# A two-part kernel on one core: each GpSimd operation also waits for the VectorE operation ahead of it in the kernel's own plan

## The chip, the core and the metric

The kernel runs on one core of a Trainium2 chip. A core has five engines with a queue of instructions each: TensorE (PE in the profile, with its weight loads as PEld), VectorE (DVE), ScalarE (ACT), GpSimd (POOL) and SyncE (SP), which here issues all DMAs. An engine takes its instructions in order and waits at an instruction until the semaphores that it names have reached given values. The metric is the device time of one execution in microseconds (us).

## The reference

The first half is a recurrence over 768 time steps, for 4 sequences of 8 heads with 48 values each; the second half is a gated feed-forward block over the result. Cut to what is computed:

```python
for t in range(S):                       # S = 768, state is D x D, D = 48
    cur = einsum('bhd,bhe->bhde', u[None] * kt, vt)
    y[:, :, t] = einsum('bhd,bhde->bhe', rt, state + cur)
    state = wt[..., None] * state + einsum('bhd,bhe->bhde', kt, vt)
x = y as [4, 768, 384]
h = gelu(x @ w_in)                       # 384 -> 1024, tanh form
u, v = h[..., :512], h[..., 512:]
v_n = (v - mean) / sqrt(var + 1e-6) * g_ln
v_s = einsum('ts,bsd->btd', w_sg, v_n) + b_sg[None, :, None]
out = x + (u * v_s) @ w_out
```

## The kernel before

The 768 steps of each of the 4 sequences are cut into 6 chunks of 128 steps, 24 chunks in all, and each chunk into two blocks of 64. Within a chunk the recurrence becomes matrix products: running products of the decays (`decays`, two scans on VectorE, L465 and L473 or L480), keys and queries multiplied by them (`decayed_k`, L505, and L482), the products of decayed queries and keys on TensorE (L563), masked on VectorE (`masked`, L640), and a state per block that is carried on (`state` and `decayed`, L654, L663, L670, L683). `own_weights` makes the term with `u`: from chunk 4 on two multiplications of 128x384 (L527, L529), a sum over them on VectorE (L532), and a product with a diagonal (L540).

The feed-forward half runs per half sequence in pieces: `v_piece` (TensorE, then a gelu on ScalarE, L863, the statistics by one-column steps L865 to L873, and the normalised piece split into a high and a low part, L882), `u_piece`, `gate_piece` (L918 to L924) and `out_piece` (L942). Products that need full precision are three TensorE matmuls, high by high, high by low and low by high (L840, L841, L842). Weights come as 64-bit numbers and are turned into high and low parts on the chip: `f64_weight` (L989, L991, L995, L997, and L1008, L1010) and `f32_weight` (L1038).

Nothing of the order is left to a scheduler. Each of these functions is a generator that yields one `Op` for each instruction or small group: the engines that may do it with a cost in us for each, what it waits for, and what it takes and frees. `Plan.run` picks, again and again, the operation that can end first by these costs, on the engine where it ends first, and lets the generator record its instructions. So the order of each queue and the choice between VectorE, GpSimd and ScalarE come from one planned timeline. An `Op` with `two=True` also uses a port that VectorE and GpSimd share in the plan (`Op.port`, `Plan.port`): in the plan such an operation on VectorE and any operation on GpSimd never overlap. On the chip nothing keeps this: an instruction waits only for its data and its buffers, and a GpSimd operation whose inputs are there starts at once, whatever VectorE was planned to do first.

Of the program that runs, GpSimd has 26 operations of preparation and then 110 that the plan places; VectorE has 571 operations.

Of the kernel before, what the change touches and what calls it, by code (L numbers as in the profile page):

```python
# [80 lines left out]
class Op:  # L81
# [3 lines left out]
    def __init__(self, on, after=(), take=(), free=(), done=None, kb=None, two=False, apart=False, small=False, slack=0.0, n=6):  # L85
        self.on, self.after, self.take, self.free, self.done, self.kb = on, after, take, free, done, kb
        self.two = two
        self.n = n
        self.slack = slack
        self.small = small  # L90
        self.apart = apart
# [6 lines left out]
class Event:  # L98
    t = None
# [36 lines left out]
class Plan:  # L136
# [4 lines left out]
    def __init__(self):  # L141
        self.engines = dict.fromkeys(("PE", "DVE", "ACT", "POOL", "SP"), 0.0)
        self.procs = []
        self.log = []
        self.dma = 0.0
        self.lanes = [0.0] * 8
        self.port = 0.0
        self.count = 0
        self.pe_last = self.pe_before = None
        self.pos, self.came = FETCH[2], [0.0, 0.0]  # L150

    def fetched(self, t, end, n):

        step = (end - t) / n
        late = 0.0
        for _ in range(n):
            self.pos += 1
            t += step
            if self.pos % 256 == 256 - FETCH[1]:
                self.came = [self.came[1], t + late + FETCH[0]]  # L160
            elif self.pos % 256 == 0:
                late += max(0.0, self.came[0] - t - late)
        return late
# [20 lines left out]
    def run(self):  # L184
        while True:
            best = {}
            for p in self.procs:
                op = p[3]
                if any(e.t is None for e in op.after) or any(len(s.free) < op.take.count(s) for s in op.take):
                    continue  # L190
                ready = max([p[2]] + [e.t for e in op.after] + [s.since(op.take.count(s)) for s in op.take])
                _, t, e = min((s + self.cost(op, e, s) + BIAS.get(e, 0.0), s, e) for e in op.on
                              for s in (max(ready, self.engines[e], self.port if op.port(e) else 0.0,
                                        self.lanes[0] if op.kb is not None else 0.0),))
                best.setdefault(e, []).append((t, p[0], p[4], p))
            if not best:
                break
            pick = None
            for e, c in best.items():
                t0 = min(x[0] for x in c)  # L200
                x = min((x for x in c if x[0] <= t0 + 0.02), key=lambda x: (x[1], x[0], x[2]))
                if pick is None or x[0] < pick[0]:
                    pick = (x[0], e, x[3])
            t, e, p = pick
            op = p[3]
            op.e, op.end = e, t + self.cost(op, e, t)
            if e == "PE":
                op.end += self.fetched(t, op.end, op.n)
            self.engines[e] = op.end
            if e == "PE":  # L210
                self.pe_before, self.pe_last = self.pe_last, op
            if op.port(e):
                self.port = op.end
            if op.kb is not None:
                self.dma = max(op.end + 1.6, self.dma) + op.kb / 330.0
                op.seen = self.dma + 0.5 + op.slack
                self.lanes = self.lanes[1:] + [self.dma + 0.5]
            else:
                op.seen = op.end + self.LAT.get(e, 0.2)
            op.got = [s.take() for s in op.take]  # L220
            for b in op.free:
                b.done(op.seen)
            if op.done is not None:
                op.done.t = op.seen
            if not op.apart:
                p[2] = op.seen
            self.log.append((t, op.end, e, p[0], p[1].__name__))
            self._next(p, op)
            if p[3] is None:
                self.procs.remove(p)  # L230
        assert not self.procs, [(p[0], p[1].__name__) for p in self.procs[:40]]
# [70 lines left out]
def rwkv_gmlp(ctx: ExitStack, tc: tile.TileContext, wpad, kr, vtok, ktok, vt, u, ucol, w_in, consts_, w_sgT, w_out, out):  # L302
    nc = tc.nc
# [84 lines left out]
    before, full, eye = (junk[:, i * 128:(i + 1) * 128] for i in range(3))  # L388
# [16 lines left out]
    plan = Plan()  # L405
    plan.engines.update(DVE=2.0, POOL=3.5, ACT=2.1, SP=0.8)
    PLANS.append(plan)
    steps = [(b, g) for b in range(B) for g in range(NC)]
    N = len(steps)

# [882 lines left out]
```

## Time and profile before

| what | value |
| --- | --- |
| median of 3 runs | 371.54 us (369.52 to 372.68) |
| the profiled execution, its own time | 372.92 us |
| its span in the profile | 371.2 us |
| busy: PE, PEld, DVE, ACT, POOL | 345.1, 312.5, 284.7, 199.6, 103.3 us |
| the chain that ended last, by engine | PE 69%, DVE 22%, issue 3%, DMA 2%, ACT 2% |

The profile is of one execution; the 1.7 us between its time and its span lie before the first and behind the last instruction of the program. Instructions are named by engine, line (L12 is line 12 of the kernel), operation and the tiles they write and read. "Idle before" names what ended the idle time of an engine just ahead of an instruction.

### The profile page before, as it was taken

To read this page: it belongs to the slowest core of one execution; us is meant where nothing else is said; L and a number is where in the kernel's file an instruction comes from. 1 tells how busy PE (TensorE), PEld (TensorE's weight loads), DVE (VectorE), ACT (ScalarE), POOL (GpSimd) and SP (SyncE) were. 2 spreads that over 40 slices of the span, in tenths; PEclk is the share of its full clock that TensorE was granted. 3 is DMA by queue.
4 is the path that set the end of the run, shared out by engine and by line. 5 is a ranking of instruction groups with operands and counts; after the bars stand their busy time and mean duration, and the time that the engine had idled before them with its cause. 6 is when DMAs were issued, how large, how long until landed. Compare 5 with 4: busy or idle time off the path is not lost.

```text
span 371.2 us, 10746 instructions
## 1 busy us (share of the span) xinstructions
PE 345.1 (93%) x4429; PEld 312.5 (84%) x4429; DVE 284.7 (77%) x571; ACT 199.6 (54%) x520; POOL 103.3 (28%) x140
## 2 busy tenths in 40 slices
PE   2899588899999999999999999999999999999991
PEld 2576367679999889989899988999999899999991
DVE  7997999999999999899999998545726354553350
ACT  2666567767644677687564577521256783521110
POOL 6221917045233564534122611121100120100000
PEclk9989999999999999999999999999999999999997
DMA  8889477542435826746346620120445431001002
GB/s 243 330 272 312 150 241 221 177 159 71 125 119 175 263 76 196 245 133 189 92 141 191 194 77 3 64 79 6 140 152 181 134 117 50 1 0 44 21 8 66
DMA packets 23432, 50.64 MB, mean 136 GB/s; under 512 B 3024, under 2 KB 11984, under 8 KB 23376
## 3 DMA queue, kind: packets, MB, share of 16 engines
q1 hardware_dynamic: 23376, 49.88, 42.2%
q8 instruction: 37, 0.61, 0.7%
q14 instruction: 19, 0.16, 0.1%
HBM read 43.97 MB, written 4.72 MB: 131 GB/s over the span
## 4 chain that ended last, share of the span: by engine, by line
PE 69%; DVE 22%; issue 3%; DMA 2%; ACT 2%; SPq 0%; DVEq 0%; ACTq 0%
PE m_ps L840 14%; PE m_ps L841 13%; PE m_ps L842 13%; PE resets L840 5%; PE resets L842 5%; PE resets L841 5%; PE a_ps L563 4%; PE y_ps L586 3%; PE y_ps L597 2%; DVE W L465 2%; PE y_ps L570 2%; DVE W L473 2%; DVE KR L505 2%; DVE a L640 1%; DMA W<-in_wpad 1%
## 5 line engine op out<-in xcount | busy, mean ns | idle before, releaser
L840 PE MATMUL m_ps<-wsgh,vn 128*128 128x384 f32 x144 | 49.4, 343 | 0.3 <-ACT u L896 0.3
L841 PE MATMUL m_ps<-wsgl,vn 128*128 128x384 f32 x144 | 48.4, 336 | 0.0
L842 PE MATMUL m_ps<-wsgh,vn 128*128 128x384 f32 x144 | 48.4, 336 | 0.0
L871 POOL TENSOR_TENSOR st<-st,mhalf 128x1 f32<-128x1 f32 x24 | 17.3, 721 | 76.4 <-DVE st L869 69.4
L491 ACT ACTIVATE junk<-W 128x1040 bf16<-128x1040 f32 x24 | 25.7, 1070 | 13.4 <-DVE W L480 5.2
L840 PEld LDWEIGHTS m_ps<-wsgh,vn 128*128 128x128 f32 x144 | 27.0, 188 | 1.6 <-ACT u L896 0.6
L840 PE MATMUL m_ps<-xT,winh 128*128 128x384 f32 x78 | 27.0, 346 | 0.6 <-ACT kt L309 0.6
L841 PEld LDWEIGHTS m_ps<-wsgl,vn 128*128 128x128 f32 x144 | 27.0, 188 | 0.5
L842 PEld LDWEIGHTS m_ps<-wsgh,vn 128*128 128x128 f32 x144 | 27.0, 187 | 0.0
L840 PE MATMUL m_ps<-g,wouth 128*128 128x384 f32 (+1 forms) x80 | 26.8, 335 | 0.0
L842 PE MATMUL m_ps<-g,woutl 128*128 128x384 f32 (+1 forms) x80 | 26.4, 330 | 0.0
L841 PE MATMUL m_ps<-g,wouth 128*128 128x384 f32 (+1 forms) x80 | 26.4, 330 | 0.0
L841 PE MATMUL m_ps<-xT,winh 128*128 128x384 f32 x78 | 26.2, 336 | 0.0
L842 PE MATMUL m_ps<-xT,winl 128*128 128x384 f32 x78 | 26.2, 336 | 0.0
L563 PE MATMUL a_ps<-KR 64*64 64x128 f32 (+1 forms) x768 | 22.9, 256 | 1.1 <-DVE S L654 1.0
L527 POOL TENSOR_TENSOR RK<-RK,flat 128x384 f32<-128x384 f32 x17 | 20.9, 1234 | 10.7 <-DVE resets L920 6.4
L922 ACT CAST g<-m_ps 128x384 fp32r<-128x384 f32 x24 | 11.4, 477 | 21.4 <-DVE m_ps L920 21.4
L586 PE MATMUL y_ps<-a,vtok 64*64 64x64 f32 x768 | 21.3, 224 | 1.1 <-DVE S L670 0.6
L842 PE MATMUL m_ps<-winh,xT 128*128 128x512 f32 x51 | 20.2, 396 | 2.3 <-ACT xT L309 2.3
L465 DVE TENSOR_TENSOR_SCAN W<-W,D 128x520 f32<-128x520 f32 x16 | 21.9, 1371 | 0.0
L586 PEld LDWEIGHTS y_ps<-a,vtok 64*64 64x64 f32 x768 | 16.1, 134 | 6.7 <-issue 3.6
L942 DVE TENSOR_TENSOR o<-m_ps,x 128x384 f32<-128x384 f32 (+1 forms) x20 | 10.4, 529 | 14.6 <-PE m_ps L842 10.3
(184 smaller groups left out, 1009.5 us busy)
## 6 DMA issues: line engine op xcount, KB each, us to landing
KR<-in_kr SPq DMA_DIRECT2D x24, 512.0 KB, 4.5
RK<-in_ktok SPq DMA_DIRECT2D x20, 384.0 KB, 3.6
W<-in_wpad SPq DMA_DIRECT2D x24, 260.5 KB, 3.0
vtok<-in_vtok SPq DMA_DIRECT2D x24, 192.0 KB, 3.4
out<-o SPq DMA_DIRECT2D x23, 192.0 KB, 1.9
vn<-in_w_in SPq DMA_DIRECT2D x6, 512.0 KB, 6.9
KR<-in_w_in SPq DMA_DIRECT2D x6, 512.0 KB, 4.3
g<-in_w_sgT SPq DMA_DIRECT2D x6, 384.0 KB, 5.4
```

What stands on the lines that cost most here:

```text
L465: nc.vector.tensor_tensor_scan(Suf[:, WL - 1:0:-1], W[:, WL - 1:0:-1], r_one if early else D1[:, WL - 1:0:-1], 0.0, ALU.mult, ALU.add)
L473: nc.vector.tensor_tensor_scan(W[:, at], W[:, at], r_two, 0.0, ALU.mult, ALU.add)
L491: nc.scalar.activation(junk.bitcast(BF16).rearrange("p (a x) -> p a x", a=2), both, AF.Square, accum_out=chk[:, n:n + 1])
L527: engine[op.e].tensor_tensor(t[:, 0], t[:, 0], u_bc, ALU.mult)
L563: nc.tensor.matmul(ps_[64 * c_:64 * c_ + 64, j, p * C:p * C + (2 * T if c_ < turn else T)], x.K[rows, at:at + T], r_, start=True, stop=True)
L586: m = nc.tensor.matmul(place(y, j, q, r, c_), x.V[64 * c_:64 * c_ + 64, h * D - up(p, j):h * D - up(p, j) + 64], x.a.tile[64 * c_:64 * c_ ...
L840: nc.tensor.matmul(ps, lh, rh, start=(i == 0), stop=False)
L841: nc.tensor.matmul(ps, lh, rl, start=False, stop=False)
L842: nc.tensor.matmul(ps, ll, rh, start=False, stop=(i == n - 1))
L871: nc.gpsimd.tensor_tensor(rstd, var, c.mhalf, ALU.pow)
L922: nc.scalar.copy(gh, ps)
L942: nc.vector.tensor_tensor(o.tile[:, 0:w], ps, h_.x.tile[:, i, at], ALU.add)
```

## The change

`Plan.run` gets two hooks: how many instructions have been recorded so far, and a function that is called after each planned operation. In the kernel this function keeps a list of all VectorE operations with their planned ends. For each planned GpSimd operation that starts at the planned time t it looks up the last VectorE operation of the list that ends by t, and adds a dependency: the first GpSimd instruction waits for that VectorE operation's last instruction. Costs, choices and the order of every queue stay as they are.

```diff
@@ Plan.__init__
+        self.behind = lambda op, n, t: None
+        self.traced = lambda: 0
@@ Plan.run
+            n = self.traced()
             self._next(p, op)
+            self.behind(op, n, t)
@@ rwkv_gmlp
+    wait = mybir.DependencyInfo(mybir.DependencyClass.Sync, mybir.DependencyReason.DATA)
+    on_dve = []
+
+    def port_order(op, n, t):
+
+        ins = nc.cur_bb.bb.instructions[n:]
+        if op.e == "DVE":
+            last = [i for i in ins if i.engine == mybir.EngineType.DVE]
+            if last:
+                on_dve.append((op.end, last[-1]))
+        elif op.e == "POOL" and ins:
+            before = [i for end, i in on_dve if end <= t + 0.01]
+            if before:
+                tc.add_manual_dep(ins[0], before[-1].name, wait, reason="port order")
+
+    plan.traced, plan.behind = lambda: len(nc.cur_bb.bb.instructions), port_order
```

In the built program the four other queues hold the same instructions in the same order with the same waits; VectorE's and TensorE's instructions update their semaphores at a few more places. On GpSimd 88 of the 110 planned operations wait for a later VectorE operation than before, and 47 more instructions that only wait stand in its queue. Seven rows of GpSimd's queue at the place that the prediction speaks of most, before; in square brackets the semaphores waited for (DVE, Activation and Pool are those of VectorE, ScalarE and GpSimd, DMAHW those of DMAs):

```order
L1038 TENSOR_TENSOR wsgl_62<-g1_414,wsgh_61 128x2x384 [waits DMAHW1_49,Activation_49]
L865 TENSOR_SCALAR st0_0_113<-st0_0_113 128x1 [waits Activation_49]
L1038 TENSOR_TENSOR wsgl_62<-g2_463,wsgh_61 128x2x384 [waits DMAHW3_49,Activation_49]
L527 TENSOR_TENSOR RK0_0_88<-RK0_0_88,flat_65 128x384 [waits DMAHW6_49,DMAHW1_49]
L529 TENSOR_TENSOR RK0_0_88<-RK0_0_88 128x384 [waits Pool_49]
L527 TENSOR_TENSOR RK1_0_89<-RK1_0_89,flat_65 128x384 [waits DMAHW7_49]
L529 TENSOR_TENSOR RK1_0_89<-RK1_0_89 128x384 [waits Pool_49]
```

The same rows of the changed kernel, whose line numbers are 20 higher:

```order
L1058 TENSOR_TENSOR wsgl_62<-g1_414,wsgh_61 128x2x384 [waits DMAHW1_49,DVE_49,Activation_49]
L885 TENSOR_SCALAR st0_0_113<-st0_0_113 128x1 [waits DVE_49,Activation_49]
L1058 TENSOR_TENSOR wsgl_62<-g2_463,wsgh_61 128x2x384 [waits DMAHW3_49,DVE_49,Activation_49]
L547 TENSOR_TENSOR RK0_0_88<-RK0_0_88,flat_65 128x384 [waits DMAHW6_49,DMAHW1_49,DVE_49]
L549 TENSOR_TENSOR RK0_0_88<-RK0_0_88 128x384 [waits DVE_49,Pool_49]
L547 TENSOR_TENSOR RK1_0_89<-RK1_0_89,flat_65 128x384 [waits DMAHW7_49,DVE_49]
L549 TENSOR_TENSOR RK1_0_89<-RK1_0_89 128x384 [waits DVE_49,Pool_49]
```

The order is the same; each row waits for VectorE now. Which VectorE operation the last five of them wait for, by the counts in the built program (line numbers of before, and the times of both in the trace of before):

| GpSimd operation | starts, before | now waits for the end of |
| --- | --- | --- |
| L1038, low part of a weight | 38.87 us | L482, 45.95 us + 0.68 |
| L527, chunk 4 | 40.68 us | L471, 47.81 us + 0.18 |
| L529, chunk 4 | 41.93 us | L505, 49.22 us + 0.68 |
| L527, chunk 5 | 43.22 us | L471, 50.44 us + 0.17 |
| L529, chunk 5 | 44.41 us | L540, 52.37 us + 0.68 |

## The prediction

> **What bounds the kernel now.** I read the page's busy strings first, then the busy times by stage, then the timelines of VectorE and GpSimd where TensorE idles. From the page (each digit is the busy share of one fortieth of the span, 9.3 us, in tenths):
>
> ```profile
> span 371.2 us, 10746 instructions
> PE   2899588899999999999999999999999999999991
> DVE  7997999999999999899999998545726354553350
> ```
>
> From slice 12 (111 us) on, TensorE is full to the end; before that it is not, and VectorE is. The same in sums, one row per stage (from:to, length, then the busy us and count of PE, PEld, DVE, ACT, POOL, the granted clock, DMA share, GB/s):
>
> ```profile
> 39.00:46.00 7.00, 3.79 (x57) 2.10 (x48) 7.00 (x9) 3.88 (x10) 6.76 (x6) 1.00 0.42 122
> 46.00:66.00 20.00, 17.05 (x344) 12.83 (x348) 19.83 (x36) 13.87 (x35) 8.24 (x12) 1.00 0.75 229
> 66.00:100.00 34.00, 32.28 (x396) 28.31 (x394) 33.97 (x73) 23.23 (x60) 10.52 (x12) 1.00 0.39 119
> 100.00:125.00 25.00, 24.35 (x457) 23.26 (x459) 24.93 (x45) 12.59 (x38) 10.57 (x11) 1.00 0.58 180
> 125.00:366.00 241.00, 237.62 (x2766) 224.50 (x2758) 164.62 (x345) 124.06 (x320) 52.79 (x61) 1.00 0.33 105
> ```
>
> From 39 to 125 us VectorE has next to no idle time, while TensorE idles 3.21 us (7.00 less 3.79), 2.95, 1.72 and 0.65: 8.53 us together. So a microsecond saved on VectorE there can become a microsecond of TensorE; behind 125 us TensorE sets the pace, and VectorE has room. What fills VectorE from 39 to 46 us, its timeline (start, duration):
>
> ```profile
> 38.96 2.04 DVE L989 TENSOR_SCALAR vn<-vn 128x512 int32<-128x512 int32 x1
> ...
> 41.19 1.22 DVE L991 SCALAR_TENSOR_TENSOR vn<-vn,vn 128x512 int32<-128x512 int32 x1
> 42.33 1.14 DVE L663 TENSOR_TENSOR S<-S,pc 128x192 f32<-128x192 f32 x1
> 43.40 1.22 DVE L995 TENSOR_SCALAR vn<-vn 128x512 int32<-128x512 int32 x1
> ...
> 44.81 1.22 DVE L997 SCALAR_TENSOR_TENSOR winl<-vn,vn 128x512 fp32r<-128x512 uint32 x1
> 45.95 0.68 DVE L482 TENSOR_TENSOR KR<-KR,W 128x512 f32<-128x512 f32 x1
> ```
>
> and the same four lines of a weight ten microseconds earlier, while GpSimd was idle or on something short:
>
> ```profile
> 27.49 0.40 DVE L989 TENSOR_SCALAR vn<-vn 128x512 int32<-128x512 int32 x1
> ...
> 29.91 0.68 DVE L991 SCALAR_TENSOR_TENSOR vn<-vn,vn 128x512 int32<-128x512 int32 x1
> ...
> 31.88 0.40 DVE L995 TENSOR_SCALAR vn<-vn 128x512 int32<-128x512 int32 x1
> ...
> 32.80 0.69 DVE L997 SCALAR_TENSOR_TENSOR winl<-vn,vn 128x512 fp32r<-128x512 uint32 x1
> ```
>
> GpSimd's timeline over the slow stretch says why:
>
> ```profile
> 38.87 1.85 POOL L1038 TENSOR_TENSOR wsgl<-g,wsgh 128x768 fp32r<-128x768 f32 x1
> 40.68 1.18 POOL L527 TENSOR_TENSOR RK<-RK,flat 128x384 f32<-128x384 f32 x1
> 41.93 1.32 POOL L529 TENSOR_TENSOR RK<-RK 128x384 f32<-128x384 f32 x1
> 43.22 1.11 POOL L527 TENSOR_TENSOR RK<-RK,flat 128x384 f32<-128x384 f32 x1
> 44.41 1.06 POOL L529 TENSOR_TENSOR RK<-RK 128x384 f32<-128x384 f32 x1
> 45.56 0.51 POOL L869 TENSOR_SCALAR st<-st 128x1 f32<-128x1 f32 x1
> ...
> 49.77 0.21 POOL L865 TENSOR_SCALAR st<-st 128x1 f32<-128x1 f32 x1 [3.70 <-ACT v L863]
> ```
>
> Each stretched VectorE operation starts just after a GpSimd operation and ends about 0.3 us after it: L989 starts at 38.96, 0.09 us behind L1038, which ends at 40.72; L989 ends at 41.00. VectorE was held until about 0.1 us before GpSimd's end and then took its own 0.40. The Trainium skill (SBUF — State Buffer, Who interferes with whom) has this as one SBUF port pair under an exclusive lock, taken for the whole instruction by whichever starts first. By that rule L989 would end at 40.72 + 0.40 = 41.12, so the trace agrees but for 0.12 us; over some nine collisions the rule would make the gain below about 1 us larger, and the sum goes by the traced durations.
>
> **The change part by part.** It takes nothing away and moves nothing on any engine. GpSimd gets later wait counts, VectorE and TensorE a few more semaphore updates, which I cost at nothing: they ride on instructions that are there already. The 47 added wait instructions stand in GpSimd's queue alone, which is busy 6.76 + 8.24 + 10.52 of the 61 us from 39 to 100, so even at 0.21 us each, the shortest GpSimd row above, the ten or so that fall there are hidden in its idle time; without that cover they would add 2 us to GpSimd's answers, which the last rival prices.
>
> *What goes: VectorE's collisions.* All five GpSimd operations that start from 38.87 to 44.41 are to wait for VectorE operations that now end at 46.63 (L482: 45.95 + 0.68) or later. So none of them can be running when L989 to L997 start. By the rows above: L989 1.64, L991 0.54, L995 0.82, L997 0.53, and L663 0.80 (1.14 less the 0.344 of a row below): 4.33 us of VectorE in a stage where TensorE idles 3.21. I count 3.21. For 46 to 100 us the groups of VectorE (count, busy us, mean ns, then idle us in front):
>
> ```profile
> L882 DVE TENSOR_TENSOR vn<-v,vn 128x512 fp32r<-128x512 f32 x6 | 4.8, 808 | 0.0
> L640 DVE COPY_PREDICATED a<-mask,a_ps 128x512 f32<-128x512 uint8 x5 | 3.6, 722 | 0.0
> L873 DVE TENSOR_TENSOR st<-st 128x1 f32<-128x1 f32 x4 | 3.1, 773 | 0.0
> L1010 DVE TENSOR_TENSOR woutl<-g 128x384 fp32r<-128x384 f32 x4 | 2.8, 703 | 0.0
> L1008 DVE TENSOR_TENSOR g<-g,wouth 128x384 f32<-128x384 f32 x4 | 2.1, 536 | 0.0
> L663 DVE TENSOR_TENSOR S<-S,pc 128x192 f32<-128x192 f32 x1 | 0.8, 827 | 0.0
> ```
>
> against the same lines from 235 to 366 us, where GpSimd does little:
>
> ```profile
> L882 DVE TENSOR_TENSOR vn<-v,vn 128x512 fp32r<-128x512 f32 x8 | 5.5, 690 | 3.8 <-ACT vn L309 3.0 <-POOL vn L309 0.8
> L640 DVE COPY_PREDICATED a<-mask,a_ps 128x512 f32<-128x512 uint8 x4 | 2.9, 728 | 0.0
> L873 DVE TENSOR_TENSOR st<-st 128x1 f32<-128x1 f32 x6 | 0.9, 152 | 0.7 <-POOL st L871 0.7
> L663 DVE TENSOR_TENSOR S<-S,pc 128x192 f32<-128x192 f32 x2 | 0.7, 344 | 0.0
> ```
>
> L640, which reads one input from PSUM, takes the same in both (722, 728): GpSimd does not hold it. The others lose 4 x 0.621 = 2.48 (L873), 6 x 0.118 = 0.71 (L882), 4 x 0.167 = 0.67 (L1010, against L1008 of the same shape) and 0.48 (L663): 4.34 us, with 4.67 us of TensorE idle beside it. I count 4.34. From 100 to 125 one collision alone
>
> ```profile
> 116.65 1.49 DVE L505 TENSOR_TENSOR KR<-KR,W 128x512 f32<-128x512 f32 x1
> ```
>
> is 0.81 above the 0.68 of that line, more than TensorE's 0.65 of idle time, so I count 0.65. Collisions behind 125 us I count at nothing: TensorE, full there, covers them; if it were not full, each would be worth its 0.5 to 0.8. Gross gain: 3.21 + 4.34 + 0.65 = 8.2 us, with 8.53 as the end that no saving on VectorE before 125 us can pass.
>
> *What comes: late answers of GpSimd.* What queues behind a waiting GpSimd operation is all of its later work. The worst place is the same stretch; the rows that decide it:
>
> ```profile
> 49.22 0.68 DVE L505 TENSOR_TENSOR KR<-KR,W 128x512 f32<-128x512 f32 x1
> ...
> 51.26 0.53 DVE L532 TENSOR_REDUCE own<-RK 128x8 f32<-128x384 f32 x1
> ...
> 52.37 0.68 DVE L540 TENSOR_TENSOR a<-own,KR 128x512 f32<-128x512 f32 x1
> ```
>
> ```profile
> 54.34 0.72 ACT L867 ACTIVATE junk<-v,st 128x512 f32<-128x512 f32 x1
> ```
>
> If VectorE stood where it stands now, L1038 would start at 46.7 (behind L482) and end at 48.6, L527 at 49.7; the first L529 waits for L505 (49.90) and ends at 51.05, just ahead of L532 at 51.26, which reads it. The second L527 ends at 52.2; the second L529 waits for L540 (53.05) and ends at 54.2. Then come the two one-column steps of the v piece, 0.51 and 0.21, until 54.9, and ScalarE's L867, which reads them, now starts at 54.34. So with operations moved by 7.8 us the reader is 0.6 us late at most. ScalarE has idle time behind it (13.87 busy of 20), so 0 to 0.6: I take 0.6.
>
> *What stays or comes new: other collisions.* A released GpSimd operation can still meet VectorE's next operation on two SBUF inputs. No row of before shows it; its bounds are none, and all of the nine or so counted above (8.2 us, nothing gained). The planner charges port time to such pairs and so puts port-free VectorE work, such as L640, behind the awaited operation; hence I take a figure near the lower end, two of nine at their mean of 0.9: 1.8 us.
>
> Sum: 8.2 - 0.6 - 1.8 = 5.8 us. The profiled execution took 372.92 us, 371.2 of span and 1.7 around it, and would take 367.1; against the median of the runs, 371.54, on which I forecast, it is **365.7 us**.
>
> **The rivals.** *The port itself is the bound (about 369.3).* If two operations can never share it, holding one back only changes which one waits. From 39 to 46 GpSimd is busy 6.76 us, and the six VectorE operations above need 0.40 + 0.68 + 0.34 + 0.40 + 0.69 + 0.68 = 3.2 unstretched: 10 us of port in a stage of 7. For it: that excess has to go somewhere, and from 46 us on GpSimd's work is 6 us longer then. Against: it goes into a stage where GpSimd is busy 8.24 of 20, and where port-free work is at hand. By it the 3.2 of the first stage and half of 4.34 are lost again: 8.2 - 5.4 - 0.6 = 2.2 us of gain. It is the Trainium skill's same section that speaks for this: an exclusive lock is time taken, not shared, whatever the order.
>
> *Something else is late next (about 369.5).* TensorE's idle time from 39 to 66 may be ended by ScalarE or a landing once VectorE is early: DMA share is 0.75 from 46 to 66. Then only the later stages pay: 2.17 of the 4.34 and 0.65, less 0.6, some 2 us. Against: VectorE has not a microsecond of idle time from 39 to 125 us, so nothing but its own queue holds it.
>
> *VectorE waits for GpSimd instead (about 378).* GpSimd runs ahead today; tied to VectorE, each of its operations begins only when VectorE arrives, and the reader, itself on VectorE, may come before it is done. GpSimd's work from 39 to 100 us is 25.5 us; VectorE now pays for it in 8.7 us of collisions (4.33 + 4.34). Where it had to sit out 15 of the 25.5 instead, the time would be 371.5 + 6.3. It is slower by over 1% only if VectorE waits for more than 8.7 + 3.7 = 12.4, half of all GpSimd work. Against it: the readers stand some operations behind the awaited one, as L532 does behind L505 (2.0 us, against the 1.06 that L529 needs).
>
> **How the numbers follow.** Chances: forecast 0.77, port 0.09, something else late 0.08, VectorE waiting 0.06. One per cent is 3.7 us, about what can be told from no change: faster is below 367.8. Of the forecast's 0.77 some 0.03 lies above that, where most collisions come back; so faster is 0.74, same 0.20, slower 0.06. The range goes from 371.54 - 8.53, with 0.2 for the runs, 362.8, up to 370.5, past the two middle rivals.
>
> **What would show it right or wrong.** Right: from 39 us on L989, L995 and L997 at 0.40 to 0.7 us, L873 at 0.15; GpSimd's five operations starting only after L482; TensorE's idle time from 39 to 66 us below 2 us; TensorE's last matmul some 6 us sooner. The port rival: the same long rows on other lines of VectorE from 46 to 66 us. The last rival: idle time of VectorE before L532, L670 or L873, released by GpSimd. Wrong at its root: collisions gone and VectorE some 8 us earlier at 125 us, but TensorE no earlier.

## The result and the profile after

The changed kernel takes 360.9 us (median of 5 runs, 359.1 to 362.49) against 372.3 us (5 runs): ratio 0.9697, 95% interval 0.9653 to 0.9741. That is 11.4 us, about twice the 5.8 us of the forecast, and below the range's lower end of 362.8 us. Run again later on one chip with the kernel before, it came to 361.06 against 370.89 us, ratio 0.9735 (0.9687 to 0.9784): 9.8 us. Its profiled execution has a span of 360.7 us, 10.5 less than before. Runs over 1.5% longer than the fastest of the same kernel are left out of every ratio here: three of the runs below, of 427.19, 387.25 and 368.66 us, and two of before.

The busy strings of the page after:

```profile
PE   2999898999999999999999999999999999999993
DVE  7998998999999998999998996465736244463251
```

TensorE is full from about 100 us on, and nearly so before, from slice 4 (36 us). The busy times by the same stages (columns as before: PE, PEld, DVE, ACT, POOL, clock, DMA share, GB/s):

```profile
39.00:46.00 7.00, 6.28 (x69) 3.86 (x68) 6.90 (x13) 4.52 (x15) 4.44 (x4) 1.00 0.74 215
46.00:66.00 20.00, 18.70 (x350) 14.55 (x348) 17.95 (x40) 15.57 (x40) 9.40 (x15) 1.00 0.80 260
66.00:100.00 34.00, 33.34 (x417) 30.45 (x420) 33.92 (x75) 24.00 (x61) 8.68 (x14) 1.00 0.33 105
100.00:125.00 25.00, 25.00 (x441) 23.56 (x432) 24.88 (x47) 13.96 (x44) 9.93 (x11) 1.00 0.69 213
```

TensorE's idle time from 39 to 66 us, 3.21 + 2.95 us before, is 0.72 + 1.30 now. VectorE's timeline at the place of the prediction's main term (line numbers are 20 higher: L1009 is L989 of before, L683 is L663):

```profile
37.40 0.40 DVE L1009 TENSOR_SCALAR vn<-vn 128x512 int32<-128x512 int32 x1
...
37.98 0.68 DVE L1011 SCALAR_TENSOR_TENSOR vn<-vn,vn 128x512 int32<-128x512 int32 x1
38.58 0.35 DVE L683 TENSOR_TENSOR S<-S,pc 128x192 f32<-128x192 f32 x1
38.85 0.42 DVE L1015 TENSOR_SCALAR vn<-vn 128x512 int32<-128x512 int32 x1
...
39.45 0.68 DVE L1017 SCALAR_TENSOR_TENSOR winl<-vn,vn 128x512 fp32r<-128x512 uint32 x1
40.05 0.69 DVE L502 TENSOR_TENSOR KR<-KR,W 128x512 f32<-128x512 f32 x1
```

The five took 2.04, 1.22, 1.14, 1.22 and 1.22 us; now they take 0.40, 0.68, 0.35, 0.42 and 0.68. GpSimd's timeline shows where its work went:

```profile
40.87 1.85 POOL L1058 TENSOR_TENSOR wsgl<-g,wsgh 128x768 fp32r<-128x768 f32 x1 [3.37 <-ACT y L313]
42.68 1.02 POOL L547 TENSOR_TENSOR RK<-RK,flat 128x384 f32<-128x384 f32 x1
44.39 1.00 POOL L549 TENSOR_TENSOR RK<-RK 128x384 f32<-128x384 f32 x1 [0.69 <-DVE KR L525]
45.35 0.99 POOL L547 TENSOR_TENSOR RK<-RK,flat 128x384 f32<-128x384 f32 x1
47.64 1.02 POOL L549 TENSOR_TENSOR RK<-RK 128x384 f32<-128x384 f32 x1 [1.29 <-DVE a L560]
```

L1058 starts behind L502 (40.05 + 0.69 = 40.74), the second L549 behind L560, as the counts said. GpSimd's own multiplications of 128x384 are shorter as well, 0.99 to 1.02 us in place of 1.06 to 1.32, which fits VectorE no longer holding them. And the groups of VectorE from 46 to 100 us:

```profile
L902 DVE TENSOR_TENSOR vn<-v,vn 128x512 fp32r<-128x512 f32 x6 | 4.1, 677 | 0.0
L660 DVE COPY_PREDICATED a<-mask,a_ps 128x512 f32<-128x512 uint8 x5 | 3.7, 731 | 0.1
L893 DVE TENSOR_TENSOR st<-st 128x1 f32<-128x1 f32 x4 | 0.6, 149 | 0.0
L1030 DVE TENSOR_TENSOR woutl<-g 128x384 fp32r<-128x384 f32 x4 | 2.2, 542 | 0.0
L683 DVE TENSOR_TENSOR S<-S,pc 128x192 f32<-128x192 f32 x1 | 0.5, 460 | 0.0
```

L893 is at 149 ns (773 before), L1030 at 542 (703), L902 at 677 (808); L660, which GpSimd did not hold before either, has not changed. Of these only L683 still meets GpSimd (460, clean 344).

To see where time was won, one number serves the rest of this section and the next: TensorE issues the same 4429 matmuls in the same order in all these kernels, so the start of the n-th of them can be compared. In the table n is the one that started at the given time in the first profile of before; each entry is its start in the other profile less that time, in us (negative is earlier). "End" is the last matmul, and the last column the stretch from its end to the end of the span.

| profile | 10 | 20 | 39 | 46 | 100 | 125 | 200 | end | behind the last matmul |
| --- | --- | --- | --- | --- | --- | --- | --- | --- | --- |
| before | 0 | 0 | 0 | 0 | 0 | 0 | 0 | 0 | 8.0 |
| before, again | 0.12 | 0.28 | 0.40 | 0.38 | 0.36 | 0.19 | 0.29 | 0.29 | 6.3 |
| changed | -0.61 | -1.76 | -1.57 | -4.71 | -7.13 | -8.01 | -9.01 | -8.48 | 6.0 |
| changed, again | 1.17 | 0.60 | -1.18 | -3.35 | -7.68 | -8.53 | -9.40 | -9.40 | 6.1 |
| first 8 waits | -0.58 | -1.72 | -1.61 | -1.60 | -0.93 | -1.10 | -1.11 | -1.11 | 6.1 |
| waits 8 to 26 | -0.44 | -0.44 | -0.45 | -3.60 | -7.02 | -7.18 | -7.10 | -7.10 | 8.1 |
| waits 27 to 48 | -0.45 | -0.53 | -0.23 | -0.21 | -1.26 | -2.19 | -1.50 | -1.40 | 8.2 |
| waits from 49 on | 0.16 | 1.30 | -0.49 | -1.58 | -1.03 | -1.75 | -2.57 | -2.49 | 6.2 |
| five waits | -0.46 | -0.21 | -1.98 | -3.49 | -5.30 | -5.99 | -6.03 | -5.16 | 5.9 |
| both ways | -0.16 | -1.30 | -1.08 | -3.37 | -6.11 | -6.60 | -7.17 | -7.18 | 6.1 |
| changed, other output buffers | -0.44 | -1.53 | -1.44 | -4.59 | -8.54 | -9.42 | -10.42 | -10.11 | 6.1 |

The start of the first matmuls varies by chance, and so does the granted clock from 20 to 39 us. In the first profile of before it was halved for 3.4 us there (the clock is the third figure from the end):

```profile
25.10:28.50 3.40, 3.40 (x32) 2.22 (x34) 2.79 (x7) 2.69 (x10) 0.82 (x1) 0.50 0.74 230
20.00:39.00 19.00, 18.17 (x336) 12.85 (x338) 16.91 (x36) 12.88 (x36) 5.87 (x8) 0.91 0.88 297
```

and in the changed kernel's second profile it was not:

```profile
20.00:39.00 19.00, 18.07 (x373) 12.96 (x372) 18.69 (x40) 13.39 (x38) 5.33 (x7) 1.00 0.91 299
```

Of the table's rows "changed, again", "waits from 49 on" and "five waits" have 1.00 from 20 to 39 us, the others 0.91. These three alone gain 1.8 us between 20 and 39, and 9% of 19 us is 1.7; the others lose up to 0.3 or stay. So each part's effect is read from differences along its row, and the -9.40 of "changed, again" holds 1.8 us of clock. From 39 us to the end the three rows with the whole change gain 6.9, 8.2 and 8.7 us.

### The profile page after: what moved, and what is told of

Same layout as the page of the kernel before. It is cut to its first block, busy times and chain, and to the rows that moved or that the text cites. A ratio compares the mean times of both kernels' runs of the same rounds, so it can differ in the third digit from the quotient of the medians.

```text
span 360.7 us, 10793 instructions
## 1 busy us (share of the span) xinstructions
PE 343.5 (95%) x4429; PEld 311.8 (86%) x4429; DVE 272.8 (76%) x571; ACT 199.4 (55%) x520; POOL 87.8 (24%) x140
## 4 chain that ended last, share of the span: by engine, by line
PE 77%; DVE 13%; DMA 3%; issue 2%; ACT 2%; POOL 1%; SPq 1%; DVEq 0%; ACTq 0%; POOLq 0%
PE m_ps L860 16%; PE m_ps L862 15%; PE m_ps L861 15%; PE resets L860 6%; PE resets L862 5%; PE resets L861 5%; PE a_ps L583 4%; PE y_ps L606 3%; PE y_ps L617 2%; PE y_ps L590 2%; DVE W L493 2%; DVE W L485 2%; DMA x<-y 1%; DVE KR L525 1%; DVE a L660 1%
## 5 line engine op out<-in xcount | busy, mean ns | idle before, releaser
L891 POOL TENSOR_TENSOR st<-st,mhalf 128x1 f32<-128x1 f32 x24 | 13.3, 553 | 74.0 <-DVE st L889 37.5
L547 POOL TENSOR_TENSOR RK<-RK,flat 128x384 f32<-128x384 f32 x17 | 17.2, 1013 | 34.4 <-DVE RK L549 5.8
L313 ACT COPY x<-y_ps 128x256 f32<-128x256 f32 (+1 forms) x38 | 11.6, 328 | 18.1 <-PE y_ps L606 15.5
L860 PE MATMUL m_ps<-winh,xT 128*128 128x512 f32 x51 | 21.0, 412 | 0.3 <-ACT v L883 0.3
L938 DVE SCALAR_TENSOR_TENSOR m_ps<-m_ps,flat 128x384 f32<-128x384 f32 x24 | 14.8, 619 | 8.4 <-PE m_ps L862 8.3
```

The costliest lines, as they stand in the source:

```text
L313: nc.scalar.copy(o, i) if e == "ACT" else engine[e].tensor_copy(o, i)
L547: engine[op.e].tensor_tensor(t[:, 0], t[:, 0], u_bc, ALU.mult)
L860: nc.tensor.matmul(ps, lh, rh, start=(i == 0), stop=False)
L891: nc.gpsimd.tensor_tensor(rstd, var, c.mhalf, ALU.pow)
L938: nc.vector.scalar_tensor_tensor(ps, ps, c.g[:, d:d + 1], c.b_bc[:, ts], ALU.mult, ALU.add)
```

## The experiments

The theory: VectorE sets the pace up to 125 us, each GpSimd operation on SBUF data that starts ahead of its turn holds VectorE's next port operation for the rest of its own time, and the change takes these collisions away, each in its own place. The main rivals: GpSimd's late answers or new collisions take much of it back; the port is full, so that order changes nothing; the gain at the end of the program is the change's too.

**The kernel before, unchanged,** and **the changed kernel, unchanged,** for second profiles.

> The kernel before once more, unchanged, for a second profile. Question: are the last 8.3 us (from the last matmul at 362.9 to the end at 371.2) a fixed cost or chance? In the first profile VectorE's last two sums waited for output DMAs (2.58 us of idle time ahead of the last), one DMA took 4.38 us, where the changed kernel's took 2.20. If the DMAs at the end take what they take by chance, the last matmul lies again at 363 us give or take 0.5, and the stretch behind it differs by 1 to 2 us from 8.3; if the change shortens it, it stays at 8.0 or more.

> The changed kernel once more, unchanged. Last matmul again 8 to 9 us earlier than in the kernel before, at 354 to 355 us. If the tail is chance, the stretch behind the last matmul is not 6.2 us again but anything from 5.5 to 8.5; if the change shortens it, it is again near 6. Time ratio 0.965 to 0.975.

Measured: 370.44 us, ratio 0.9989 (0.9956 to 1.0022), and 361.06 us, 0.9735 (0.9687 to 0.9784). The kernel before ended 6.3 us behind its last matmul this time, not 8.0; the changed one 6.1. VectorE's last two rows in the first profile of before, and in the second:

```profile
363.06 0.36 DVE L942 TENSOR_TENSOR o<-m_ps,x 128x192 f32<-128x192 f32 x1 [1.59 <-DMA out<-o]
366.00 0.36 DVE L942 TENSOR_TENSOR o<-m_ps,x 128x192 f32<-128x192 f32 x1 [2.58 <-DMA out<-o]
```

```profile
363.27 0.36 DVE L942 TENSOR_TENSOR o<-m_ps,x 128x192 f32<-128x192 f32 x1 [1.52 <-DMA out<-o]
363.96 0.36 DVE L942 TENSOR_TENSOR o<-m_ps,x 128x192 f32<-128x192 f32 x1 [0.33 <-DMA out<-o]
```

The same wait for an output DMA was 2.58 us once and 0.33 once. In the table the last stretch takes about 6 or about 8 us, with no wait added and with some. So 2.0 of the 10.5 us between the two first spans can be chance, and the shift of the last matmul, 8.5 and 9.4 us, is the better measure of the change. That the whole change makes the long end rarer is not excluded: none of its profiles has it.

**The wait on some of the GpSimd operations alone.** Each planned GpSimd operation gets a number k, from 0 to 109 in the plan's order:

```diff
-    on_dve = []
+    on_dve, placed = [], []
@@ port_order
         elif op.e == "POOL" and ins:
+            placed.append(op)
+            k = len(placed) - 1
             before = [i for end, i in on_dve if end <= t + 0.01]
-            if before:
+            if before and k < 8:          # and 8 <= k < 27, 27 <= k < 49, k >= 49, 10 <= k < 15
```

> The added wait on the first 8 planned GpSimd operations alone (those that start before 36 us). If what counts is the collision of each stage: L989 at 12.7 us, held 1.0 us by L482 on GpSimd, is freed, and TensorE's matmuls at 39 us and later stand 0.6 to 1.2 us earlier than before, no more; time 0.997. If the early 1.6 us of the changed kernel came from landings that happened to be early: 0 us. If holding GpSimd back works by something else than these collisions (the early order of all later work), much more, 3 us and over.

Measured: 370.01 us, 0.9975 (0.9939 to 1.001), which the times alone can't tell from nothing. The profile can: VectorE's two L1011 (L989 of before) at the place of the first collision, here and in before:

```profile
11.82 0.73 DVE L1011 TENSOR_SCALAR vn<-vn 128x512 int32<-128x512 int32 x2
```

```profile
12.40 1.72 DVE L989 TENSOR_SCALAR vn<-vn 128x512 int32<-128x512 int32 x2
```

1.0 us is freed, and TensorE moves by 1.14 us between 10 and 20 (-0.58 to -1.72). The changed kernel, the one "both ways" and the one with other output buffers show the same step (-1.15, -1.14, -1.09), and of the five profiles without these waits none moves earlier there by more than 0.1 ("waits from 49 on" moves 1.1 later, at other matmuls). Nearer to the collision nothing is left to chance: the matmul that waits for VectorE's next line, L991, started at 14.87 us in before, an earlier one, which does not wait for it, at 12.90. Between these two the shift changes by -0.98 or -0.99 us in all six profiles with these waits, the changed kernel's second one and the third last operation's below included, and by 0.00 or 0.01 in the five others. At 39 us, among the profiles with the lowered clock, the rows with these waits stand at -1.08 to -1.61 and those without at 0.40 to -0.45, so the gain has lasted till then. In the row of "first 8 waits" it shrinks behind 46 us; this profile alone has a granted clock of 0.79 from 39 to 46 us and 0.90 to 66.

> The wait on planned GpSimd operations 8 to 26 alone (those that start from 36.9 to 64.1 us in the trace of before). Collisions: 4.3 us are freed from 39 to 46 and 2.2 to 3.0 from 46 to 66, so TensorE at 66 us stands 4.4 to 6 us earlier, and that stays to the end: time 0.984 to 0.988. If VectorE's saving were lost to late answers of GpSimd or to new collisions (my deduction of 2.4 us), 3 to 4 us.

Measured: 366.78 us, 0.9888 (0.9853 to 0.9923). TensorE moves from -0.45 at 39 to -6.33 at 66 us: 5.9 us, at the upper end of the 4.4 to 6 expected, and it is 6.6 us at 100. By time it is 4.1 us (2.9 to 5.5), between what was expected and the 3 to 4 of the rival, which the times alone do not reject. The profile is one execution, and why the two measures differ was not found.

> The wait on planned GpSimd operations 27 to 48 alone (those that start from 70 to 124 us in the trace of before). Collisions freed there: 0.7 and 0.8 us on L1010 and L873 to 100 us, and three of 0.4 to 0.8 to 125 us; TensorE's idle time there is 1.72 and 0.65 us in all, and some of it is not VectorE's. So TensorE at 125 us stands 0.7 to 2 us earlier than at 66 us, time 0.995 to 0.998. If the parts only work together (VectorE must be early already), 0.

Measured: 369.34 us, 0.9935 (0.9897 to 0.9972). From 46 to 125 some 2.0 us (-0.21 to -2.19), of which 0.8 is given back behind 125, where TensorE is full: 1.2 stay. By time it is 1.8 us, so the parts do not need each other.

> The wait on planned GpSimd operations from 49 on alone (those that start behind 125 us). TensorE is full there in the kernel before, so collisions freed are covered: TensorE's last matmul 0 to 0.5 us earlier. If collisions matter there too because VectorE's results gate TensorE now and then, 0.5 to 1.0. If the added wait holds GpSimd's answers back in the stage that TensorE fills, later than before by up to 1 us.

Measured: 370.64 us, 0.998 (0.9939 to 1.0021): the times decide nothing. TensorE moves from -1.75 at 125 to -2.49 at the end, 0.7 us earlier, within the second of the three expected cases. The 0.7 between 100 and 125 in the same row has no added wait in it, so a change of that size can be chance; that these waits gain is likely, not shown.

> The wait on five GpSimd operations alone, those of the prediction's main term (L1038, L527, L529, L527, L529, which start from 38.87 to 44.41 us in the trace of before). If the term was right, 4.3 us of VectorE are freed and TensorE, idle 3.2 us from 39 to 46, stands 3.2 to 4.3 us earlier at 66 us, and the same to the end: time 0.988 to 0.992. If their late answers or collisions elsewhere took part of it (the deduction of 2.4 us), 1 to 2.5 us. If the port is full there (first rival), under 1 us.

Measured: 367.63 us, 0.9919 (0.9885 to 0.9954). From 39 to 100 TensorE moves from -1.98 to -5.30: 3.3 us. That is the term as it stood in the prediction (4.33 freed, 3.21 counted), without any deduction; "waits from 49 on", with the same clock and no added wait there, moves by 0.5 in the same stretch. By time it is 3.1 us (1.7 to 4.3), which alone rejects the port rival but not the deductions.

**A wait for the third last VectorE operation** in place of the last:

```diff
             before = [i for end, i in on_dve if end <= t + 0.01]
+            before = before[:-2]
             if before:
```

> Every planned GpSimd operation waits, but for the third last VectorE operation ahead of it in the plan, not the last: GpSimd cannot run ahead by microseconds, yet it can start one or two VectorE operations early. If it is the run-ahead that costs, nearly all of the gain stays (9 us, 0.975). If each collision is with the operation just ahead, whatever the distance, a large part is lost: collisions come back on VectorE's lines, and 2 to 5 us are left (0.987 to 0.995).

Measured: 364.02 us, 0.9833 (0.9787 to 0.9878): of 9.8 us 6.2 remain by the ratio, 7.1 by the medians. Its profile is of the longest of its five executions, so it is not in the table and serves for single rows alone. The timelines of VectorE and GpSimd show what the two operations of slack cost:

```profile
39.91 0.68 DVE L1018 SCALAR_TENSOR_TENSOR winl<-vn,vn 128x512 fp32r<-128x512 uint32 x1
40.51 2.34 DVE L503 TENSOR_TENSOR KR<-KR,W 128x512 f32<-128x512 f32 x1
```

```profile
40.13 2.17 POOL L1059 TENSOR_TENSOR wsgl<-g,wsgh 128x768 fp32r<-128x768 f32 x1 [2.32 <-ACT winh L1035]
```

L1059 is now free to start during L1018, two operations early, and L503 takes 2.34 us in place of 0.69. Neither expectation fits alone: running ahead by microseconds accounts for the greater part of the gain, and the operation just ahead for a quarter to a third.

**Both ways:** VectorE's port operations also wait for the GpSimd operation planned ahead of them.

```diff
+            if op.two and last:
+                ahead = [i for end, i in on_pool if end <= t + 0.01]
+                if ahead:
+                    tc.add_manual_dep(last[0], ahead[-1].name, wait, reason="port order")
...
+            on_pool.append((op.end, ins[-1]))
```

> The changed kernel, and each VectorE operation that uses the port in the plan also waits for the GpSimd operation planned ahead of it: the two never overlap in either direction. If what is left of collisions in the changed kernel costs something, this is no better, since VectorE then waits where it was held before: VectorE's rows are never stretched but idle ahead instead, and a wait is some 0.1 us longer than a collision; last matmul 0.5 to 2 us later than in the changed kernel. If GpSimd being held by VectorE costs in the changed kernel, a gain of up to 1 us over it.

Measured: 364.33 us, 0.9838 (0.9794 to 0.9881), slower than the change alone, and the last matmul 1.3 to 2.2 us later than in the changed kernel's two profiles. Who VectorE waited for from 39 to 125 us (us in total, times, longest), here:

```profile
DVE W L505 <- POOL RK L552: 0.6, 1, 0.6
DVE KR L530 <- POOL RK L552: 0.3, 1, 0.3
...
DVE a L565 <- POOL RK L554: 0.3, 1, 0.3
```

and in the changed kernel, all of it:

```profile
DVE st L889 <- ACT junk L887: 1.8, 1, 1.8
```

So in the changed kernel no wait of VectorE for GpSimd is listed in that stage. With both ways there are seven, 2.3 us in all, where the stretched rows that remain in the changed kernel lose 1.4 us (listed in the next section): making VectorE wait is a loss.

**Other buffers for the last output piece,** on top of the change:

```diff
-        op = yield Op({"DVE": 0.06 + 0.42 / parts}, take=[s_o], free=[m, h_.x])
+        op = yield Op({"DVE": 0.06 + 0.42 / parts}, take=[s_v2 if parts == 2 else s_o], free=[m, h_.x])
```

> The changed kernel, and the last piece of output (two halves) takes its two output buffers from those of the v piece, which are free by then, so VectorE's last two sums no longer wait for output DMAs. Seven profiles so far end either some 6.1 or some 8.1 us behind the last matmul (before 8.0, then 6.3 with the same kernel), by how long one output DMA takes. If VectorE's wait for the buffer carries that to the end, the stretch behind the last matmul is 5 to 5.8 us every time, and the time 0.7 to 2.8 us below the changed kernel's: ratio to before 0.962 to 0.972. If the late DMA itself is what the end waits for, the two lengths stay.

Measured: 360.75 us, 0.9728 (0.9683 to 0.9774), the same as the change alone. VectorE's last operation no longer waits for a DMA:

```profile
353.12 0.36 DVE L962 TENSOR_TENSOR v<-m_ps,x 128x192 f32<-128x192 f32 x1 [0.31 <-PE m_ps L862]
```

but the stretch behind the last matmul is 6.1 us, not 5 to 5.8. My expectation failed. One part of it held: the second of the four output DMAs, which took 4.3 to 4.4 us in every profile with a long end, took 3.97 us here, and the end was short all the same. Whether the 8 us case is gone, one profile can't say.

## Why the prediction was wrong in size

The direction, the mechanism and the place were right: the gain is VectorE's collisions with GpSimd, most of it from 39 to 66 us, at the instructions and durations that were named. The size was not, by about half of the measured gain. Step by step:

**The main term, 3.21 us from 39 to 46.** Right. The five waits alone move TensorE by 3.3 us, some of it behind 46 us.

**4.34 us from 46 to 100 and 0.65 to 125.** Right as gross figures: the changed kernels' three profiles show 2.4, 4.3 and 4.0 us from 46 to 100 (-4.71 to -7.13, -3.35 to -7.68, -4.59 to -8.54), and 0.9 each from 100 to 125. The 2.4 has a cause of its own. In that profile one DMA of `x` took 4.45 us, where the same one took 2.23 and 2.40 in the two others, and ScalarE and TensorE stood still until it landed at 61.99 (TensorE's row names no releaser, but L849 reads the same `x`):

```profile
62.05 0.51 ACT L313 CAST xT<-x 128x384 fp32r<-128x384 f32 x1 [2.27 <-DMA x<-y]
62.08 0.88 PE L849 MATMUL m_ps<-x,same 128*128 128x384 f32 x2 [1.30 <-issue]
```

VectorE's 1.8 us in front of L889, shown above, is the same wait one step on: it waits for ScalarE's L887, which stands behind that cast. So the second rival, a landing that is late next, came true in one profile of three, for under 2 us. For 100 to 125 us the reading was wrong, though the cap hid it: it names one collision, and there were three, with 2.0 us together. The other two are

```profile
114.15 2.00 DVE L465 TENSOR_TENSOR_SCAN W<-W,D 128x520 f32<-128x520 f32 x1
123.41 0.78 DVE L683 TENSOR_TENSOR S<-S,pc 128x192 f32<-128x192 f32 x1
```

against 1.22 and 0.34 alone.

**The deductions, 0.6 for late answers and 1.8 for new collisions.** Too large: this is the first step that failed. Gross, I had 8.2 us from 39 to 125; the three profiles show 6.4, 7.3 and 8.0, mean 7.3, where I forecast 5.8; the 6.4 is the profile with the late DMA. The late answer came nearly as worked out. ScalarE's row in the changed kernel:

```profile
49.39 0.72 ACT L887 ACTIVATE junk<-v,st 128x512 f32<-128x512 f32 x1 [0.51 <-POOL st L885]
```

It waits 0.51 us for GpSimd, where I had 0.6, and 0.52 and 0.51 in the two other profiles. In these two the gross gain from 46 to 100 us is there all the same (4.3 and 4.0), so ScalarE's room covered at least most of it. New collisions exist, too, such as VectorE's L500 in the changed kernel, held by a GpSimd L547 that ran from 109.40 to 110.41:

```profile
109.79 1.71 DVE L500 TENSOR_TENSOR_SCAN W<-W,D 128x520 f32<-128x520 f32 x1
```

That is 0.5 above the 1.22 that this line (L480 of before) takes alone, but at 110 us TensorE is full now, and it costs nothing that can be seen. In the stage where collisions cost something, 39 to 100 us, the changed kernel's rows lose 0.5 us (L525 at 43.33 takes 0.91 us for 0.68, L485 at 75.33 1.41 for 1.22, L683 0.46 for 0.34), and 0.9 us from 100 to 125, where I had deducted 1.8. I had put a fixed share of collisions against the gain without asking in which stage they would fall.

**A sum that began at 39 us.** The second step that failed, and the plainest. The L989 of 12.40 us had lost 1.0 us to the GpSimd operation of 12.56 and was in none of my rows, since I started at 39 us, although VectorE is busy for 9.76 of the 10 us from 10 to 20. It is worth 1.0 to 1.1 us to TensorE.

**Nothing behind 125 us.** Small, but not nothing: 0.5, 0.9 and 0.7 us in the three profiles.

These add up: 1.1 + 7.3 + 0.7 = 9.1 us by TensorE's matmuls, against 8.5, 9.4 and 10.1 at the end of the three rows, which hold the chance of the first microseconds and of the clock as well.

**The range's lower end, 362.8.** It took 8.53 us, TensorE's idle time from 39 to 125, as the most that could be gained. That is the cap of a stage, used as the cap of the program; 1.8 us came from outside it. Most of what is left up to the 11.4 us by the first medians I can't assign: the end of the program takes 2 us more or less by one DMA, the clock of 20 to 39 us gives or takes 1.8, and the medians of before lie between 370.4 and 372.3. By the later medians, 9.8 us, little is left.

**The rivals.** The port was not full: GpSimd is busy 2.3 us less from 39 to 46 us and 1.2 more from 46 to 66 (9.40, 8.24 before); part of its work moved into the stage behind, and part of its time was its own stretching. Nothing else late next took the gain: TensorE's idle time fell from 6.16 to 2.02 us from 39 to 66, with the one late DMA above among what is left. From 39 to 125 us no wait of VectorE for GpSimd is listed.

The Trainium skill (SBUF — State Buffer, Who interferes with whom) says that a VectorE instruction with two SBUF inputs contends with a GpSimd instruction that reads SBUF, that one with at most one SBUF input (outside VectorE's two-port modes) does not, and that whichever issues first has the shared pair for its whole instruction. The traces agree with a correction: L503, with two SBUF inputs, was held for 1.65 us, and L660, whose data are in PSUM, was not (731 ns). But by the profile's times the pair is free about 0.1 us before GpSimd's end: L1059 ended at 42.30, L503 at 42.85, 0.55 later and not the 0.69 that it takes.

## What to carry to other kernels

Where VectorE sets the pace and GpSimd helps it, a GpSimd operation whose inputs come early is not free: it takes the shared port as soon as they are there. Look for rows of VectorE that take a second or third length beside their usual one, and make GpSimd wait for the VectorE operation that should go first; the reverse wait was not worth having here. When the gain is summed up, start the sum at time zero, and use the idle time of a stage as a cap for that stage alone. And compare the granted clock of two profiles stage by stage before a shift between them is called an effect.

## What was not expected of the hardware

The output DMA whose buffer VectorE's last operation waits for took 4.38, 2.06, 2.20 us in three profiles of two kernels that issue it alike, and in the eleven profiles of the table the stretch behind the last matmul was 5.9 to 6.3 us or 8.0 to 8.2, with nothing between (8.5 in the twelfth, not in the table). It was long in those where this DMA took 4.3 us or more. The late DMA of `x` shows the same difference in size, 2.2 us. What makes one DMA late was not tried.

The granted clock was 0.50 for 3.4 us once between 20 and 39 us in nine of the twelve profiles and not at all there in three, of the changed kernel in one profile and not in the other. By the table this moved TensorE by 1.8 us.

Two slack operations in the order cost a quarter to a third of the gain: a port that is taken 0.4 us too early (L1059 at 40.13, L503 at 40.51) held VectorE for 1.65 us.
